# Decay attention, mixture of experts and bilinear layer on one core: where y is summed, where the T sums are formed, how 64-bit weights are staged

## The chip, the cores and the metric

One NeuronCore of a Trainium2 chip runs the whole chain. The metric is device time in microseconds (us) of the core. The engines are PE (matrix products, with PEld its weight loads), DVE (vector), ACT (scalar), POOL (GpSimd) and SP, which here issues nearly all DMAs. Each engine works through its own instructions in the order in which the program gives them; semaphores order the engines against each other.

## The reference

```python
attn_out = _attn_ref(q, k, v, lam)                 # (2, 8, 768, 64), blocked decay attention
x = attn_out.transpose(0, 2, 1, 3).reshape(1536, 512)
# mixture of experts, E = 4, F = 1024: w1 (4, 512, 1024), w2 (4, 1024, 512)
p = domain_probs / (domain_probs.sum(-1, keepdims=True) + 1e-09)
for e in range(4):
    out += p[:, e:e+1] * (np.maximum(x @ w1[e], 0.0) @ w2[e])
# bilinear layer: w1, w2 (512, 1024), w3 (1024, 1024), w_out (1024, 512)
h = (x @ w1) * (x @ w2) @ w3
return h @ w_out
```

`w1`, `w2`, `w3` and `w_out` of the last layer come as 64-bit floats (`1.0 / np.sqrt(...)` makes them so), all else as 32-bit.

## The kernel before

**Numbers in two parts.** Every operand of a product is split into a high part (fp32r, an ACT cast) and a low part (what is left, a DVE subtract), and each product is three matmuls: high by low, low by high, high by high (`products`, L111). A matmul is 128x128 weights by 512 columns.

**Three groups of tokens.** The 1536 tokens are three groups of 512 (`TG`). Hidden units are taken in 32 blocks `k` of 128 (`NJ`), 8 for each expert.

- Attention runs first, with the first blocks of group 0 mixed in; the order is the list `ORDER`, which ends with block 7 in hand.
- **Phase one** (loop at L922) takes group 0 through blocks `k` = 8 to 29: `moe_in(k)` (12 matmuls into bank 4 + k % 3), `moe_z` (DVE), `moe_high` (ACT), then `moe_out(k-2)` (12 matmuls into banks 0 to 3, where group 0's y is summed), `moe_low` (DVE). Blocks 30 and 31 are mixed into the first passes of phase two.
- **Phase two** (loop at L940) takes groups 1 and 2 together, two blocks (a pair `n`) in each pass `m`. Seven products of Strassen's kind (`MULT`, L712) of 6 matmuls each stand for the eight that two groups by two blocks would need. They use sums of x (`x_sums`, L641, POOL, once) and the **T sums** of w1 (`pair_sums`, L661, four POOL instructions for a pair). Between the products stand eight packs of 6 matmuls that bring the hidden units to y. Even passes serve group 1 or 2 in turn (`pass_packs`, L779): four y banks (0 to 3) are summed over two pairs and then added by DVE to a sum in SBUF (`to_sum`, L806), or copied the first time. Products use banks 4 to 6 as chains A, B, C, bank 7 is the w bank in phase one.
- **Gates and the rest** (L968 on): (x w1) * (x w2) of the last layer, again with Strassen-like products for groups 1 and 2 (`quad`), and then by W = w3 w_out (`final`).

**64-bit weights** are converted by hand (`begin64`, `bits64`, `end64`, L228 to L249): two ACT passes, three DVE passes, one POOL add, then the split. The 24 tiles of w_out and w3 are converted in phase one, four w_out tiles, eight w3 tiles, and again, and `w_block` (L588) makes W by 12 matmuls a tile into bank 7: the first eight blocks are copied out by ACT (`w_part`), the second eight added to them by DVE (`w_sum`, L600) and stored in DRAM. The raw tile comes through the pool `raw` of three buffers that all weights share, the converted one through `cv` of two.

**The order of work around the change** is a table of steps: `at_step(t, rank, what, call)` puts a call at position `t`, and `step(t)` emits it there. In phase one 100 units of `t` are one block `k`, in phase two 100 units are a pass and one unit one product or pack. A call that names a tile (`what`) frees a raw buffer, and the next tile of `stream` is loaded behind it (`load_next`, L617), so loads stand on SP's queue in the order in which buffers come free.

## Time and profile before

| | |
|---|---|
| runs | 939.7, 943.1, 950.19 us; median 943.1 us |
| profiled execution | 942.55 us, of which the span of the trace is 940.8 us |
| PE, DVE, ACT, POOL busy | 828.4, 562.7, 333.4, 212.2 us |
| DMA | 88.81 MB, mean 94 GB/s |

A busy PE is not PE at its peak: a matmul record lasts some 390 ns while the next begins after 227 ns, and at a lower granted clock it lasts longer. So the count of matmuls in a stretch, not its busy time, says how long it could have been.

### The profile page before, as it was taken

How to read it: one execution, taken by the hardware profiler on the slowest of the kernel's cores; microseconds unless marked ns; L12 is line 12 of the kernel's file. 1: busy time of each engine (PE TensorE's matmuls, PEld its weight loads, DVE VectorE, ACT ScalarE, POOL GpSimd, SP SyncE). 2: the span in 40 equal slices, each digit the busy share in tenths (PEclk: the TensorE clock that was granted, in tenths of full speed). 3: DMA queues.
4: the chain of work that ended last, by engine and by line, in shares of the span. 5: the costliest groups of instructions: out<-in, count | busy, mean ns of one | idle time of the engine just before them, and what ended most of it. 6: DMA issues, size and time to landing. Idle time of an engine off the chain costs nothing.

```text
span 940.8 us, 10423 instructions
## 1 busy us (share of the span) xinstructions
PE 828.4 (88%) x3968; PEld 666.1 (71%) x3968; DVE 562.7 (60%) x803; ACT 333.4 (35%) x574; POOL 212.2 (23%) x175
## 2 busy tenths in 40 slices
PE   8999928779377699999999999999998689999998
PEld 7778816558255488777777777777787478888887
DVE  6653574245542557766776667777766575677610
ACT  4541433334421234544333333343333433244311
POOL 2111251011110122232222222222200041178200
PEclk9999959899787999999999999999999899999999
DMA  7881333223332322433222222222223310100001
GB/s 257 269 283 46 121 114 106 73 90 107 127 114 87 116 86 68 143 95 106 93 90 79 86 82 90 79 90 79 79 79 99 136 57 10 45 1 1 0 38 53
DMA packets 39938, 88.81 MB, mean 94 GB/s; under 512 B 4560, under 2 KB 9936, under 8 KB 39888
## 3 DMA queue, kind: packets, MB, share of 16 engines
q1 hardware_dynamic: 39216, 88.12, 28.7%
q8 instruction: 31, 0.51, 0.2%
q14 instruction: 19, 0.16, 0.1%
q10 hardware_dynamic: 672, 0.03, 0.0%
HBM read 77.62 MB, written 10.51 MB: 94 GB/s over the span
## 4 chain that ended last, share of the span: by engine, by line
PE 49%; DVE 21%; ACT 9%; issue 4%; DMA 3%; POOL 0%; ACTq 0%; POOLq 0%; DVEq 0%
PE y L122 12%; PE h L734 8%; PE o L122 7%; PE w L122 7%; PE ab L122 4%; PE a L1162 4%; PE b L1162 4%; DVE z L749 4%; PE h L122 4%; DVE w L105 3%; DVE zp L758 3%; DVE z L747 2%; ACT zp L754 2%; DMA raw<-in_w3t_dram 2%; DVE cv L219 1%
## 5 line engine op out<-in xcount | busy, mean ns | idle before, releaser
L122 PE MATMUL y<-zp,w 128*128 128x512 f32 x768 | 198.5, 404 | 27.7 <-DVE ya L812 25.4
L122 PEld LDWEIGHTS y<-zp,w 128*128 128x128 f32 x768 | 147.0, 193 | 66.0 <-DVE ya L812 32.6
L226 POOL TENSOR_TENSOR cv<-cv,raw 128x512 uint32<-128x512 uint32 x40 | 53.2, 1331 | 434.5 <-issue 224.6
L754 ACT CAST zp<-z 128x512 fp32r<-128x512 f32 x64 | 39.7, 621 | 186.1 <-DVE z L749 186.1
L122 PE MATMUL w<-wol,w3h 128*128 128x512 f32 x64 | 36.0, 563 | 70.0 <-ACT w3h L102 30.1
L105 DVE TENSOR_TENSOR wl<-raw,wh 128x1024 fp32r<-128x1024 f32 (+1 forms) x33 | 42.8, 1297 | 53.9 <-ACT wh L102 53.9
L122 PEld LDWEIGHTS w<-wol,w3h 128*128 128x128 f32 x64 | 16.8, 263 | 79.9 <-ACT w3h L102 31.0
L316 ACT CAST hh<-z 128x512 fp32r<-128x512 f32 x32 | 19.8, 619 | 139.3 <-DVE z L309 139.3
L758 DVE TENSOR_TENSOR zp<-z,zp 128x512 fp32r<-128x512 f32 x64 | 58.2, 928 | 11.7 <-ACT zp L754 11.6
L122 PE MATMUL o<-w_hi,z 128*128 128x512 f32 (+1 forms) x208 | 60.0, 373 | 0.0
L309 DVE SCALAR_TENSOR_TENSOR z<-h,pb 128x512 f32<-128x512 f32 x32 | 22.0, 688 | 57.0 <-PE h L122 56.7
L122 PE MATMUL y<-hl,wh 128*128 128x512 f32 x128 | 50.7, 396 | 1.1 <-DVE hl L322 1.1
L122 PE MATMUL h<-xl,wh 128*128 128x512 f32 x128 | 51.4, 402 | 0.0
L122 PE MATMUL h<-xh,wl 128*128 128x512 f32 x128 | 50.1, 391 | 0.0
L122 PE MATMUL y<-hh,wl 128*128 128x512 f32 x128 | 50.0, 390 | 0.0
L122 PE MATMUL y<-hh,wh 128*128 128x512 f32 x128 | 49.9, 390 | 0.0
L747 DVE TENSOR_TENSOR z<-h,u 128x512 f32<-128x512 f32 x32 | 21.9, 685 | 45.3 <-ACT u L741 45.3
L102 ACT CAST wh<-raw 128x1024 fp32r<-128x1024 f32 (+1 forms) x33 | 33.6, 1018 | 38.8 <-PE y L122 35.7
L122 PEld LDWEIGHTS o<-w_hi,z 128*128 128x128 f32 x208 | 38.1, 189 | 6.9
L105 DVE TENSOR_TENSOR w<-w,w 128x512 fp32r<-128x512 f32 x32 | 30.7, 960 | 19.4 <-ACT w L102 19.4
L749 DVE SCALAR_TENSOR_TENSOR z<-z,pb 128x512 f32<-128x512 f32 x48 | 40.4, 842 | 1.6
L122 PE MATMUL o<-w_lo,z 128*128 128x512 f32 (+1 forms) x104 | 38.2, 373 | 0.0
(220 smaller groups left out, 1778.8 us busy)
## 6 DMA issues: line engine op xcount, KB each, us to landing
w<-in_w_dram SPq DMA_DIRECT2D x32, 512.0 KB, 4.0
raw<-in_w_dram SPq DMA_DIRECT2D x31, 512.0 KB, 3.8
raw<-in_w3t_dram SPq DMA_DIRECT2D x16, 512.0 KB, 3.2
raw<-in_wab_dram SPq DMA_DIRECT2D x16, 512.0 KB, 3.2
raw<-in_wout_dram SPq DMA_DIRECT2D x8, 512.0 KB, 3.2
ab_dram<-cv SPq DMA_DIRECT2D x16, 256.0 KB, 4.8
ab<-ab_dram SPq DMA_DIRECT2D x8, 512.0 KB, 3.7
kv<-in_kv_dram SPq DMA_DIRECT2D x7, 512.0 KB, 5.4
```

The lines of the kernel that those rows point to most:

```text
L102: act.copy(out=hi, in_=src)
L105: eng.tensor_tensor(out=lo, in0=src, in1=hi.bitcast(F32), op=ALU.subtract)
L122: lambda i=i, a=a, b=b: pe.matmul(ps, a, b, start=(first and i == 0), stop=(last and i == n - 1))
L226: pool.tensor_tensor(out=b, in0=b, in1=raws.pop(("f", i))[:, :, 0], op=ALU.add)
L309: dve.scalar_tensor_tensor(out=z, in0=h_ps.pop(k)[0], scalar=0.0, in1=pb_t[k // KF, 0], op0=ALU.max, op1=ALU.mult)
L316: act.copy(out=hh, in_=h_t[k][0])
L734: pe.matmul(chain_ps[to], w, x, start=begins and j == 0, stop=j == len(seq) - 1, skip_group_check=True,)
L747: dve.tensor_tensor(out=z, in0=src, in1=kept_u[name], op=ALU.add)
L749: dve.scalar_tensor_tensor(out=z, in0=src, scalar=0.0, in1=pb_t[2 * n // KF, PAIR[m]], op0=ALU.max, op1=ALU.mult)
L754: act.copy(out=t[:, 0], in_=z)
L758: dve.tensor_tensor(out=t[:, 1], in0=z_of.pop((m, f)), in1=t[:, 0].bitcast(F32), op=ALU.subtract)
L1162: pe.matmul(t, w, x, start=i == 0 and n in (1, 2, 5), stop=i == len(seq) - 1, skip_group_check=True,)
```

## The change

- **y of one group in PSUM.** In phase two group 1's y is summed in banks 0 to 3 over all 16 pairs (`first_pass`) and split from there once at the end (`first_split`). Group 2's y has banks 4 and 5, first for its column blocks 0 and 1, then for 2 and 3, each time over two pairs, then added in SBUF as before (`second_pass`, in the even passes). The products have banks 6 and 7, two chains A and B. There are 17 passes in place of 18. Passes 0 and 1 have four packs each, the last one twelve and no products. Gates turn through four pairs of banks.
- **T and x sums on DVE.** The T sums are formed in place, and those of the first 8 pairs in phase one: a tile of w1 is loaded into one buffer of its own (`xt`), summed, stored in DRAM, and read back in phase two as one more tile through `raw` (`"t"`). `x_sums` becomes eight half-size DVE instructions.
- **Conversions staged.** The 24 tiles of w_out and w3 have a raw pool (`r64`, 3) and a converted pool (`ct`, 3) of their own and a stream of their own; all of w_out comes first, into tiles that stay. Begin, bits, high, low and the product stand at least 25 units apart. W is summed over both halves in bank 7 (24 matmuls) and copied once by ACT. All 32 blocks of group 0 now go in phase one, which steps every 25 units; casts and subtracts that stood in one call are separate steps, in both phases.

The core of the diff:

```diff
...
-    f64 = []
-    for q in range(2):
-        f64 += [("wo", mt, q, wout[mt]) for mt in range(4 * q, 4 * q + 4)]
-        f64 += [("w3", kt, q, w3t[kt, q]) for kt in range(KF)]
+    f64 = [("wo", mt, mt // 4, wout[mt]) for mt in range(KF)]
+    f64 += [("w3", kt, q, w3t[kt, q]) for kt in range(KF) for q in range(2)]
     f64 += [("ab", i, q, wab[i, q]) for i in range(KF) for q in range(2)]
 
     spill = {
         "w": tc.dram_tile([P, KF, DM], F32, name="w_dram"),
         "ab": tc.dram_tile([KF, P, 2 * DM], F32, name="ab_dram"),
         "y0": tc.dram_tile([P, KD, TG], F32, name="y0_dram"),
+        "t": tc.dram_tile([NJ // 2, P, 2 * DM], F32, name="t_dram"),
...
+            place, tag = (r64_p, "r64") if i < 24 else (raw_p, "raw")
+            t = place.tile([P, 512, 2], U32, tag=tag, name="raw64")
...
+        place, tag = (ct_p, "ct") if i < 24 else (cv_p, "cv")
+        singles[i] = place.tile([P, 512], F32, tag=tag, name="cv")
...
-    cv_p = opened(ctx, "cv", 2)
     early = ExitStack()
-    wp_p = opened(early, "wp")
+    wo_p = opened(early, "wo")
     xs_p = opened(early, "xs")
     ws_p = opened(early, "ws", 2)
+    ct_p = opened(early, "ct", 3)
+    xt_p = opened(early, "xt")
+    r64_p = opened(early, "r64", 3)
...
-        for call in products(ps, pairs):
+        for call in products(w_ps[kt], pairs, first=q == 0, last=q == 1)[6 * half : 6 * half + 6]:
             call()
 
-    def w_sum(kt, q):
-        if q == 0:
-            w_part[kt] = wp_p.tile([P, DM], F32, tag=f"w{kt}", name="w_part")
-            act.copy(out=w_part[kt], in_=w_ps.pop(kt))
-        else:
-            t = ws_p.tile([P, DM], F32, tag="ws", name="w_sum")
-            dve.tensor_tensor(out=t, in0=w_ps.pop(kt), in1=w_part.pop(kt), op=ALU.add)
-            sp.dma_start(out=spill["w"][:, kt], in_=t)
+    def w_sum(kt):
+        w_part[kt] = ws_p.tile([P, DM], F32, tag="ws", name="w_sum")
+        act.copy(out=w_part[kt], in_=w_ps.pop(kt))
+
+    def w_store(kt):
+        sp.dma_start(out=spill["w"][:, kt], in_=w_part.pop(kt))
...
-    SPLIT_A = NJ - 2
-    PAIRS = 100 * SPLIT_A
-    GATES = PAIRS + 100 * (NP + 2)
+    NPRE = 8
+    PAIRS = 100 * NJ
+    GATES = PAIRS + 100 * (NP + 1)
...
+        dve.tensor_tensor(out=x_sum[n][:, d], in0=left[:, d], in1=right[:, d], op=op)
...
+        f = raws["w1", n] if n >= NPRE else early_w1[n]
+        both, b12, b22 = f[:, 0], f[:, 1, : 2 * P], f[:, 1, 2 * P :]
+        t1, t4 = f[:, 0, : 2 * P], f[:, 0, 2 * P :]
+        dve.tensor_tensor(out=both, in0=f[:, 1], in1=both, op=ALU.subtract)
+        dve.tensor_tensor(out=t4, in0=t1, in1=t4, op=ALU.subtract)
+        dve.tensor_tensor(out=b12, in0=b22, in1=b12, op=ALU.subtract)
+        dve.tensor_tensor(out=b22, in0=b22, in1=t1, op=ALU.subtract)
+
+    early_w1 = {}
+
+    def early_load(n):
+        if n < NPRE:
+            t = early_w1[n] = xt_p.tile([P, 2, DM], F32, tag="t", name="w1")
+            sp.dma_start(out=t, in_=w12[2 * n : 2 * n + 2, :, :DM].rearrange("f p c -> p f c"))
+
+    def early_store(n):
+        sp.dma_start(out=spill["t"][n], in_=early_w1.pop(n).rearrange("p q n -> p (q n)"))
...
+        7: ("s3", "t3", "B"),
         3: ("s4", "b22", "A"),
-        4: ("a22", "t4", "C"),
+        4: ("a22", "t4", "B"),
...
+            chain_ps[to] = bank(6 + "AB".index(to), "h")
...
+    def out_pack(g, n, f, half, first, last):
+        zh, zl = z_pair[n, g, f][:, 0], z_pair[n, g, f][:, 1]
+        wh, wl = w2_t[n, f]
+        for d in (2 * half, 2 * half + 1):
+            if first:
+                y_ps[g, d] = bank((d, 4 + d % 2)[g], "y")
+            c = slice(d * P, (d + 1) * P)
+            for call in products(y_ps[g, d], [((wh[:, c], wl[:, c]), (zh, zl))], first=first, last=last):
+                call()
+
+    def first_pass(ns):
+        return [
+            (lambda n=n, f=f, half=half: out_pack(0, n, f, half, n == 0 and f == 0, n == NP - 1 and f == 1), None)
+            for n in ns
+            for f in range(2)
+            for half in range(2)
+        ]
+
+    def second_pass(ns):
+        of = [(n, f) for n in ns for f in (1, 0)]
+        return [
+            (
+                lambda j=j, n=n, f=f, half=half: out_pack(1, n, f, half, j == 0, j == len(of) - 1),
+                (lambda half=half: [to_sum(d, ns[-1] == NP - 1) for d in (2 * half, 2 * half + 1)])
+                if j == len(of) - 1
+                else None,
+            )
+            for half in range(2)
+            for j, (n, f) in enumerate(of)
+        ]
+
+    def to_sum(d, last):
+        if d not in yacc:
+            yacc[d] = h_p.tile([P, TG], F32, tag="hh" if d < 3 else "hl", name="ya")
+            act.copy(out=yacc[d], in_=y_ps[1, d])
+        else:
+            dve.tensor_tensor(out=yacc[d], in0=y_ps[1, d], in1=yacc[d], op=ALU.add)
         if last:
             if d == 0:
-                y_t[g] = features(g, "y")
-            split(yacc[g, d], *y_t[g][d])
+                y_t[2] = features(2, "y")
+            split(yacc[d], *y_t[2][d])
+
+    def first_split():
+        y_t[1] = features(1, "y")
+        for d in range(KD):
+            split(y_ps[0, d], *y_t[1][d])
...
+        at_step(100 * (j - 3) + 60, 0, None, lambda j=j: prep_high(j))
+        at_step(100 * (j - 3) + 76, 0, ("j", j), lambda j=j: prep_low(j))
     for i in range(24):
         what, n, q, _ = f64[i]
-        t = 100 * KF + 50 * (i * 4 // 3) + 100 * (i // 12)
+        t = 808 + 95 * i if i < 8 else 1568 + 68 * (i - 8)
         at_step(t, 3, None, lambda i=i: begin64(i))
-        at_step(t + 50, 2, ("f", i), lambda i=i: bits64(i))
-        at_step(t + 100, 1, None, lambda i=i: end64(i))
+        at_step(t + 50, 2, None, lambda i=i: bits64(i))
+        at_step(t + 75, 9, ("f", i), lambda: None)
+        at_step(t + 125, 3, None, lambda i=i: end64(i, False))
+        at_step(t + 150, 4, None, lambda i=i: end64(i, True))
         if what == "w3":
-            at_step(t + 150, 4, None, lambda n=n, q=q: w_block(n, q))
-            at_step(t + 200, 5, None, lambda n=n, q=q: w_sum(n, q))
-    at_step(1000, 6, None, x_sums)
+            at_step(t + 225, 6, None, lambda n=n, q=q: w_block(n, q, 0))
+            at_step(t + 250, 6, None, lambda n=n, q=q: w_block(n, q, 1))
+            if q:
+                at_step(t + 251, 1, None, lambda n=n: w_sum(n))
+                at_step(t + 325, 9, None, lambda n=n: w_store(n))
...
+        at_step(1800 + 50 * i, 7, None, lambda n=n, d=d: x_sums(n, d))
...
+    for n in range(NPRE):
+        t = 1800 + 120 * n
+        if n == 0:
+            at_step(t - 75, 8, None, lambda: early_load(0))
+        at_step(t, 8, None, lambda n=n: pair_sums(n))
+        at_step(t + 1, 9, None, lambda n=n: early_store(n))
+        at_step(t + 60, 9, None, lambda n=n: early_load(n + 1))
...
+            at_step(t, 1, None, lambda n=n: pair_first(n, False))
+            at_step(t + 2, 1, None, lambda n=n: pair_first(n, True))
+            at_step(t + 2, 2, None, lambda n=n: pair_second(n, False))
+            at_step(t + 3, 1, ("w1", n, 1) if pre else None, lambda n=n: pair_second(n, True))
+            if not pre:
+                at_step(t + 4, 1, None, lambda n=n: pair_sums(n))
+            at_step(t + (4 if pre else 5), 2, None, lambda n=n: pair_split(n, False))
+            at_step(t + 6, 2, ("t", n) if pre else ("w1", n, 1), lambda n=n: pair_split(n, True))
+        at_step(t + 5, 3, None, lambda n=m: pair_out(n, 0, False))
+        at_step(t + 6, 3, None, lambda n=m: pair_out(n, 0, True))
+        at_step(t + 11, 3, None, lambda n=m: pair_out(n, 1, False))
+        at_step(t + 12, 3, ("w2", m), lambda n=m: pair_out(n, 1, True))
...
+        at = t + (2 + 2 * n if n < 4 else 100 + n - 4)
...
+    at_step(t + 9, 0, None, lambda: first_split())
...
-    for k in range(n_in, SPLIT_A):
+    for k in range(n_in, NJ):
         for part in range(2):
             moe_in(k, part, 4 + k % 3)
+            if part == 0:
+                step(100 * k)
         moe_z(k)
         moe_high(k)
-        step(100 * k)
+        step(100 * k + 25)
         if k - 2 >= n_out:
             for part in range(2):
                 moe_out(k - 2, part)
+                if part == 0:
+                    step(100 * k + 50)
         moe_low(k)
-        step(100 * k + 50)
-        if k == 27:
+        step(100 * k + 75)
...
+            fill = left_over(NJ - 2) + left_over(NJ - 1)
+        elif m == NP:
+            tail = second_pass((m - 2, m - 1))
+            fill = tail[:4] + first_pass((m - 1,)) + tail[4:]
+        elif m % 2:
+            fill = first_pass(tuple(n for n in (m - 2, m - 1) if n >= 0))
+        else:
+            fill = second_pass((m - 2, m - 1))
...
+            for at, i in zip((0, 1, 3, 5, 7, 9, 10) if m > 1 else (0, 1, 3, 5, 6, 8, 9), MULT):
...
+            t = bank(((6, 7), (4, 5), (0, 1), (2, 3))[i % 4][q], f"ab{q}")
...
```

## Rows read from the trace of the kernel before

**Rows 1.** The page: busy times; PE and its granted clock in 40 slices.

```profile
PE 828.4 (88%) x3968; PEld 666.1 (71%) x3968; DVE 562.7 (60%) x803; ACT 333.4 (35%) x574; POOL 212.2 (23%) x175
...
PE   8999928779377699999999999999998689999998
...
PEclk9999959899787999999999999999999899999999
```

**Rows 2.** Stages: length, busy us (x instructions) by engine, PEclk, DMA share, GB/s.

```profile
94.00:355.00 261.00, 189.16 (x721) 148.93 (x720) 130.48 (x177) 87.58 (x132) 49.28 (x32) 0.86 0.31 103
355.00:756.00 401.00, 366.17 (x1538) 294.53 (x1537) 280.05 (x387) 150.75 (x258) 87.79 (x77) 0.97 0.29 92
756.00:940.80 184.80, 181.59 (x816) 150.88 (x816) 99.20 (x126) 59.08 (x106) 59.15 (x40) 0.99 0.08 26
```

**Rows 3.** PE's waits, 94 to 355 us: total us, times, longest.

```profile
PE w L122 <- ACT w3h L102: 30.1, 2, 17.5
PE w L122 <- DVE w_sum L606: 19.1, 5, 4.6
PE w L122 <- ACT w_part L603: 16.4, 7, 3.5
```

**Rows 4.** PE's waits after it, 355 to 757 us.

```profile
PE y L122 <- DVE ya L812: 25.4, 17, 2.5
PE ab L122 <- DVE ya L812: 4.7, 1, 4.7
```

**Rows 5.** The chain of waits: start us, us, what.

```profile
755.83 39.81 PE ab L122 x168
795.64 21.76 PE o L122 x96
```

**Rows 6.** DVE groups, 110:352 us: xcount, busy us, mean ns, idle.

```profile
L322 DVE TENSOR_TENSOR hl<-z,hh 128x512 fp32r<-128x512 f32 x18 | 17.3, 963 | 0.8 <-ACT hh L316 0.7
L219 DVE SCALAR_TENSOR_TENSOR cv<-raw,cv 128x512 uint32<-128x512 uint32 x22 | 15.2, 692 | 0.8
L309 DVE SCALAR_TENSOR_TENSOR z<-h,pb 128x512 f32<-128x512 f32 x19 | 13.1, 688 | 46.6 <-PE h L122 46.6
L210 DVE TENSOR_SCALAR cv<-cv 128x512 f32<-128x512 f32 x22 | 11.4, 517 | 0.0
L105 DVE TENSOR_TENSOR w3l<-cv,w3h 128x512 fp32r<-128x512 f32 x16 | 11.0, 689 | 13.2 <-ACT w3h L102 13.2
L214 DVE TENSOR_SCALAR cv<-cv 128x512 uint32<-128x512 uint32 x22 | 9.4, 427 | 0.8
...
L105 DVE TENSOR_TENSOR a22l<-xf,a22h 128x1024 fp32r<-128x1024 f32 x1 | 1.2, 1227 | 2.5 <-ACT a22h L102 2.5
```

**Rows 7.** DVE's time line beside POOL's x sums: start us, us, instruction.

```profile
121.38 3.35 DVE L105 TENSOR_TENSOR wl<-raw,wh 128x1024 fp32r<-128x1024 f32 x1
```

**Rows 8.** DVE's groups, 400 to 700 us (phase two).

```profile
L758 DVE TENSOR_TENSOR zp<-z,zp 128x512 fp32r<-128x512 f32 x53 | 47.9, 923 | 9.6 <-ACT zp L754 9.6
...
L812 DVE TENSOR_TENSOR ya<-y,ya 128x512 f32<-128x512 f32 x48 | 29.7, 680 | 0.0
...
L105 DVE TENSOR_TENSOR wg<-w,wg 128x256 fp32r<-128x256 f32 x13 | 5.4, 419 | 0.0
```

**Rows 9.** PE's time line, phase two: start us, us, instruction [idle <-releaser].

```profile
516.15 2.60 PE L122 MATMUL y<-zp,w 128*128 128x512 f32 x6 [1.82 <-DVE ya L812]
```

**Rows 10.** DMAs: xcount, KB, us to landing; last, of 40:94 us.

```profile
w<-in_w_dram SPq DMA_DIRECT2D x32, 512.0 KB, 4.0
...
ab_dram<-cv SPq DMA_DIRECT2D x16, 256.0 KB, 4.8
...
w_dram<-w_sum SPq DMA_DIRECT2D x8, 256.0 KB, 3.9
...
y_dram<-y SPq DMA_DIRECT2D x4, 256.0 KB, 2.6
...
raw<-in_w_dram SPq DMA_DIRECT2D x5, 512.0 KB, 6.4
```

303 lines of the change are left out of this document (138 added, 165 removed).

## The prediction

> **What bounds the kernel now.** I read the page first, then three stages, then PE's waits in each. The page has PE busy for 88% of the span and its clock below full in many slices [rows 1]; busy time hides both, so I count matmuls. The price of one at full clock is in the chain of waits: 96 matmuls of the last product in 21.76 us [rows 5], 0.2267 us each. By stage [rows 2]:
>
> - 94 to 355 us (phase one from block 8): 721 matmuls would take 163.4 us; it took 261.0. Lost: 97.6 us, at a mean granted clock of 0.86.
> - 355 to 756 us (phase two): 1538 would take 348.7; it took 401.0. Lost: 52.3 us, at 0.97.
> - 756 us to the end: 816 would take 185.0; it took 184.8. Nothing is lost.
>
> So PE's work is the floor, 150 us are lost above it, and the last stage shows that the other engines can keep PE full.
>
> In phase one the three longest waits come to 65.6 us, and all are waits of the product that makes W: for its converted w3 tile, and for bank 7 to be emptied by ACT or DVE [rows 3]. The rest of the 97.6 is mostly the clock, lower after such stops. Conversions stand in one call with their casts, behind other work in ACT's and DVE's queues, on raw buffers shared with everything. In phase two the 17 waits for `ya` (25.4 us) and one of 4.7 at the first gates [rows 4] are y banks that DVE has not yet added out. A stop of 1.82 us is followed by six matmuls in 2.60 us [rows 9] where 1.36 would do, so each costs more than its wait.
>
> **The change part by part.** The number of matmuls stays. So I take off both losses, 97.6 + 52.3 = 149.9 us, and add what I expect to be lost in the new order.
>
> *Conversions staged.* One position unit is worth 1/100 block: 24 matmuls, 5.44 us, and where w3 is converted, every 68 units, also 12 more (2.72 us), so 100 units are 9.44 us. From the low part (t+150) to its product (t+225) are 75 units, 7 us, for one cast and one subtract of 0.69 [rows 6]. From bank 7's copy (t+251) to the next block's first matmul (t+361) are 110 units, 10 us, for one ACT copy. Both waits of [rows 3] should go. The eight `w_sum` adds go (8 x 0.68). New pools cost SP nothing but the first tile, whose buffer is free only when attention's tiles are: I put 3 us, between 0 and one load, 4.0 [rows 10], and it is ACT that waits there.
>
> *DVE in phase one.* After the change: 22 weight subtracts of 1.23, 24 z and 24 low parts of 0.69, 24 conversions of 0.52 + 0.43 + 0.69 + 0.69, 7 x subtracts of 1.23, 8 x sums of 0.69, 8 T sums, the first pair 2.3 us [rows 6]. A T sum is one 128x512 and three 128x256 instructions; the trace has them on POOL only, so I take DVE's subtracts of those shapes, 0.69 + 3 x 0.42 = 1.95 [rows 6, 8]. Sum: 147 us beside 768 matmuls of PE, 174.1 us. The densest part is t = 1800 to 2640, 79 us of PE: 21.9 (weights, z, low) + 28.8 (conversions) + 15.6 (T) + 5.5 + 4.9 = 77 us of DVE. That is 97%, less for the overlap of neighbouring instructions. PE need not stop when DVE is late by less than about 6 us, since hl(k) is used two blocks on; I put 5 us for stops here, between 0 and 20.
>
> *T sums through DRAM.* One buffer: sum, store 512 KB, load 512 KB, next sum, every 120 units, 11.3 us. The sum waits at the head of DVE's queue, and z, low parts and conversions stand behind it; SP's wait for the store holds the weight loads behind it. No row has a store of 512 KB: 256 KB took 2.6, 3.9 and 4.8 us; a load took 4.0, and 6.4 in the busy stretch [rows 10]. The trip is 1.95 + 2.6 + 4.0 = 8.6 us at the least and 1.95 + 9.6 + 6.4 = 18 at the most (a store of twice 4.8). I take 4.8 and 5.0, since traffic here will be high (four 512 KB transfers or so in each 11 us): 11.8 us. Seven trips cost 7 x (11.8 - 11.3) = 3.5, I put 4; ends 0 and 47. The Trainium skill (SBUF — State Buffer, "The DMA setup-cost knee") gives about 2 us fixed plus bytes at 436 GB/s, an estimate of 3.2 us for 512 KB either way. By it the trip is 8.4 us and these 4 us are nothing; the rows above, longer, decide for me.
>
> *POOL relieved.* DVE's 128x1024 subtract of 1.23 took 3.35 us while POOL formed the x sums [rows 7], and in phase two low parts mean 0.92 where 0.69 is their price [rows 8, 6]. With T and x sums on DVE these stretches go; that is in the DVE sums, not counted again.
>
> *Phase two.* A steady pass is 90 matmuls, 20.4 us. DVE has seven z instructions, four low parts, weight subtracts (0.69, 0.42, 1.23, 2 x 0.69) and a conversion (1.64): 13.0 us; an even pass four `ya` adds of 0.68, 15.7; from pair 8 on a T sum, 17.6. All below 20.4. In odd passes no y bank turns at all. In even passes banks 4 and 5 must be added out between half 0 (step 8) and half 1 (step 11), two products or 2.72 us for two adds, 1.36, behind a z that ends about then. Eight turns: I put 0.75 us each with the clock, 6 us. Ends 0 and 30, the latter by today's wait and its slow matmuls, 1.82 + 1.24 + some, 3.7 each [rows 9]. In passes 0 to 6 a fourth tile goes through three raw buffers: w2 is loaded at step 3, when w1 is freed, and cast at step 5, so ACT waits some 2 us for its 4.0 us landing; u copies stand ahead of it and PE has two packs in hand, so nothing. Passes 0 and 1 have 66 matmuls, 15.0 us, for 13 us of DVE in a chain: 2 us each, 4. The last pass drains group 2's second half and the splits under four packs and the first gate: 4 us, 0 to 10.
>
> *Gates.* Four weight preparations move behind the first gate; DVE is busy for 99 of 185 us there, so nothing; four pairs of banks take the 4.7 us wait and the slow start of the gates away.
>
> Sum: 940.8 - 149.9 + (3 + 5 + 4) + (6 + 4 + 4) = 816.9 us of span, and 1.75 outside it (942.55 - 940.8): 819 us. The profiled run stands 0.55 us below the median of 943.1, so against the median I say **820 us**.
>
> **Rivals.**
>
> 1. *The T trip sets the pace* of t = 1800 to 2640. For it: one buffer, a store that must land before the load, DVE at 97%. Against: loads are otherwise 4.0 us. At 15 us a trip, 7 x 3.7 = 26 in place of 4: 842 us. Chance 0.13.
> 2. *Half turns of two y banks.* Before, four banks turned at each pass and PE waited 17 times; now two turn inside a pass. At today's price, 30 in place of 6: 844 us. The Trainium skill (Perfetto Trace Analysis, "Optimizing Tensor Performance", "Matmuls") wants independent groups to rotate through different banks, so that one is emptied while the next is filled; banks 4 and 5 do not. The trace agrees as far as its waits for `ya` go. Chance 0.12.
> 3. *Phase one stays bound by latency.* bank 7 and the one w3 pair stay, and ACT's and DVE's queues stay in order; if waits move to z or hl, half of the 97.6 us is lost again: 868 us. For it: 97% of DVE. Against: from 94 to 118 us, the fifth slice, conversions ran at a closer spacing beside a PE that was full at full clock [rows 1]. Chance 0.12.
> 4. *Slower.* The DVE queue, stopped by each T load, holds z, hl and the conversions, and the 8 pairs come one by one. To lose the 123 us that I expect to win, a trip must take 11.3 + 123/7 = 29 us: a store and a load of 13 us each, twice the longest of [rows 10]. At 32 us it is 820 + 7 x 20 = 960 us. Chance 0.04.
> 5. *It does not do what it says*: the new pools overlay memory whose release comes late, so that the first tiles wait and everything shifts with little gain: half of all losses stay, 893 us; 0.03, and with no gain at all 943 us, 0.02.
>
> **How the numbers follow.** My case has 0.54. Its own range is 806 (its added losses nearly nothing: the floor of 790.9 plus 1.75 is 793, and some stops always remain) to 838. The range of 8 in 10 takes in rivals 1, 2 and 3: 806 to 872. A change below 1% can't be told from none here. Faster by over 1%: 0.54 + 0.13 + 0.12 + 0.12 + 0.03, less something for mishaps of which I know nothing: 0.92; same 0.03; slower 0.05.
>
> **What would show it.** Phase one after attention near 186 us for 768 matmuls at a clock near full; no wait of PE for w3 or bank 7 above 10 us in total; stores and loads of t of 4 to 6 us each and DVE waiting under 1 us for a T load; odd passes of 20.4 us and even ones under 22; no wait for `ya` over 1 us but in even passes; the first gate without a stop. Wrong if PE waits for z's bank or hl in phase one, if DVE's longest releaser there is the DMA of w1, or if PE waits at step 11 of the even passes.

## The result: 802.3 us where 820 was forecast

The changed kernel takes 802.34 us, the median of four runs (801.64 to 803.04); the kernel before, run beside it, took 942.26 us (939.7 to 950.19; a fourth run, 941.42 us, moved its median from 943.1). The ratio is 0.850, with an interval of 0.845 to 0.855. The forecast of a gain through both stages holds; the time lies 18 us below the forecast and 4 us below the low end of its range, 806.

### The profile after

The page of the kernel after, its span, busy times, and PE's slices and clock, against [rows 1]:

```profile
span 801.3 us, 10423 instructions
...
PE 788.7 (98%) x3968; PEld 645.3 (81%) x3968; DVE 554.0 (69%) x835; ACT 332.2 (41%) x570; POOL 148.9 (19%) x107
...
PE   9999999999899999999999999999999999999998
...
PEclk9999999999999999999999999999999999999999
```

The count of matmuls is the same 3968. The slices that were below 9 in [rows 1], eight between the sixth and the fourteenth and three near the 32nd, are gone but for one, the eleventh, at 8, and so is the lower clock. DVE, which got POOL's sums, is busy for 554 us, no longer than before. In phase two its low parts of z, 0.92 us in the mean of [rows 8], are back at their price, by the page's row after:

```profile
L800 DVE TENSOR_TENSOR zp<-z,zp 128x512 fp32r<-128x512 f32 x64 | 44.1, 689 | 17.9 <-ACT zp L796 16.5
```

That is not the T sums' move alone. With only them on DVE, in the kernel before (a run below), the same low parts still mean 0.87 us; and in the kernel after the low parts of w2 mean 1.15. By DVE's groups, 400 to 600 us, of that run and then of the kernel after:

```profile
L758 DVE TENSOR_TENSOR zp<-z,zp 128x512 fp32r<-128x512 f32 x39 | 33.2, 868 | 6.9 <-ACT zp L754 6.9
```

```profile
L105 DVE TENSOR_TENSOR w<-w,w 128x512 fp32r<-128x512 f32 x20 | 22.9, 1147 | 2.7 <-ACT w L102 2.7
```

The only work that POOL has there in either is its add for the conversion. It now falls beside another DVE instruction than before.

The stages of the kernel after (length, busy us and instructions of PE, PEld, DVE, ACT and POOL, PEclk, DMA share, GB/s), cut at the first high by high matmul of phase two and at the first gate, against [rows 2]:

```profile
93.90:279.00 185.10, 177.94 (x772) 145.20 (x771) 154.30 (x216) 89.56 (x137) 39.66 (x24) 0.99 0.56 187
279.00:611.90 332.90, 332.90 (x1463) 273.59 (x1462) 240.05 (x371) 142.26 (x242) 31.64 (x16) 1.00 0.36 117
611.90:801.30 189.40, 185.95 (x841) 154.20 (x839) 106.83 (x137) 64.56 (x113) 61.55 (x40) 1.00 0.10 35
```

By the price of [rows 5], 0.2267 us, and the kernel's own counts (768, 1464 and 840; the records at the cuts differ by a few), the floors are 174.1, 331.9 and 190.4 us. So phase one loses 11.0 us, phase two 1.0, and the rest is 1.0 shorter than its count. (Phase two's first matmul stands 0.45 us ahead of the cut: cut there, it is 10.6 and 1.5.) Before, 97.6 and 52.3 us were lost. The rest can be shorter than its count because 48 of its matmuls have only 256 columns and follow each other after 0.12 us; by that its floor is some 5 us lower, here as in [rows 2], and what it spends above it is mostly the 3.2 us behind the last matmul.

PE's waits over the whole span (total us, times, longest), against [rows 3, 4]:

```profile
PE w L122 <- ACT w_sum L614: 5.2, 3, 3.2
PE w L122 <- DVE w3l L105: 1.9, 2, 1.5
```

The 65.6 us of waits for w3 and bank 7 are 7.1; the 17 waits for `ya` and the one at the first gate are gone altogether.

The chain of waits after (start us, us, what): the last four packs of passes 4, 5, 8 and 9, and the end of phase two:

```profile
364.73 5.44 PE y L122 x24
...
385.13 5.44 PE y L122 x24
...
446.62 5.48 PE y L122 x24
...
467.20 5.44 PE y L122 x24
...
590.34 21.76 PE y L122 x96
612.10 43.08 PE ab L122 x190
```

From pass 4 on these packs stand 20.40 to 20.58 us apart, where 90 matmuls are 20.4: 20.40 in passes without a T sum, 20.53 to 20.58 in those with one; the last 96 y matmuls take exactly the 21.76 us of [rows 5], and the gates begin at the moment they end.

### The profile page after: what moved, and what is told of

It reads as the page before. It is cut to its first block, busy times and chain, and to the rows that moved or that the text cites. A ratio compares the mean times of both kernels' runs of the same rounds, so it can differ in the third digit from the quotient of the medians.

```text
span 801.3 us, 10423 instructions
## 1 busy us (share of the span) xinstructions
PE 788.7 (98%) x3968; PEld 645.3 (81%) x3968; DVE 554.0 (69%) x835; ACT 332.2 (41%) x570; POOL 148.9 (19%) x107
## 4 chain that ended last, share of the span: by engine, by line
PE 80%; DVE 12%; DMA 5%; issue 1%; ACT 1%; SPq 0%; POOL 0%; ACTq 0%; DVEq 0%; POOLq 0%
PE y L122 27%; PE h L776 19%; PE o L122 8%; PE h L122 5%; PE ab L122 5%; PE a L1236 5%; PE b L1236 5%; DMA w<-in_w_dram 3%; DVE wl L105 2%; PE a L525 2%; PE a L442 2%; DVE hl L331 2%; PE a L519 1%; PE w L122 1%; DVE w3l L105 1%
## 5 line engine op out<-in xcount | busy, mean ns | idle before, releaser
L122 PE MATMUL y<-zp,w 128*128 128x512 f32 x768 | 186.3, 389 | 0.0
L122 PEld LDWEIGHTS y<-zp,w 128*128 128x128 f32 x768 | 144.0, 188 | 30.3 <-ACT ya L855 0.2
L227 POOL TENSOR_TENSOR cv<-cv,raw 128x512 uint32<-128x512 uint32 x40 | 71.3, 1782 | 434.2 <-DVE cv L220 402.2
L800 DVE TENSOR_TENSOR zp<-z,zp 128x512 fp32r<-128x512 f32 x64 | 44.1, 689 | 17.9 <-ACT zp L796 16.5
L789 DVE TENSOR_TENSOR z<-h,v 128x512 f32<-128x512 f32 x16 | 11.0, 690 | 43.5 <-ACT wf L102 29.4
L318 DVE SCALAR_TENSOR_TENSOR z<-h,pb 128x512 f32<-128x512 f32 x32 | 21.9, 685 | 18.8 <-PE h L122 18.3
L122 PE MATMUL h<-xh,wh 128*128 128x512 f32 x128 | 34.8, 390 | 0.0
L791 DVE SCALAR_TENSOR_TENSOR z<-z,pb 128x512 f32<-128x512 f32 x48 | 33.2, 692 | 1.7
L331 DVE TENSOR_TENSOR hl<-z,hh 128x512 fp32r<-128x512 f32 x32 | 28.8, 900 | 5.2 <-ACT hh L325 5.2
```

The source lines that it names most:

```text
L122: lambda i=i, a=a, b=b: pe.matmul(ps, a, b, start=(first and i == 0), stop=(last and i == n - 1))
L227: pool.tensor_tensor(out=b, in0=b, in1=raws.pop(("f", i))[:, :, 0], op=ALU.add)
L318: dve.scalar_tensor_tensor(out=z, in0=h_ps.pop(k)[0], scalar=0.0, in1=pb_t[k // KF, 0], op0=ALU.max, op1=ALU.mult)
L331: dve.tensor_tensor(out=hl, in0=z, in1=hh.bitcast(F32), op=ALU.subtract)
L791: dve.scalar_tensor_tensor(out=z, in0=src, scalar=0.0, in1=pb_t[2 * n // KF, PAIR[m]], op0=ALU.max, op1=ALU.mult)
L800: dve.tensor_tensor(out=t[:, 1], in0=z_of.pop((m, f)), in1=t[:, 0].bitcast(F32), op=ALU.subtract)
```

## The experiments

Times are medians of four runs (ten for the x sums on DVE); the ratios are to the kernel before, run beside each (its medians were 935 to 942 us). The kernel after was not run beside them, so a difference of 1 or 2 us from its 802.3 says little. "Phase one" is the length from 93.9 us to the first high by high matmul of phase two in the profiled execution; it is 185.1 us in the kernel after, and its floor is 174.1.

### The T sums in phase one

**A control.** One buffer fewer for the raw 64-bit tiles, which the next experiment needs for its room.

```diff
-    r64_p = opened(early, "r64", 3)
+    r64_p = opened(early, "r64", 2)
...
```

> The changed kernel with two raw buffers for the 64-bit tiles in place of three; the control of the next run. The changed kernel took 802.3 us with a span of 801.3. Theory A (what is lost in phase one is lost to the round trip of the single T buffer, whose sums start 12.4 us apart where 11.3 were planned): two buffers still leave 61 position units, some 5.7 us, for a load of 3.3 to 3.8 us, so 802 to 804. Theory B (DVE, busy for 17 to 20 of each 20 us from 100 to 240 us, is the bound): 802 to 804 too. Rival C (the own raw buffers are what keeps phase one fed): over 810.

803.6 us (ratio 0.856, 0.850 to 0.863), phase one 186.2 us. That is 1.3 us more, within the spread of the runs (802.4 to 804.6): the third buffer is worth next to nothing.

**Two buffers for the T tiles** (and the control's edit), so that the next tile of w1 is loaded 120 units earlier.

```diff
-    xt_p = opened(early, "xt")
+    xt_p = opened(early, "xt", 2)
...
-        at_step(t + 60, 9, None, lambda n=n: early_load(n + 1))
+        at_step(t - 60, 9, None, lambda n=n: early_load(n + 1))
```

> The run before plus a second T buffer, each load issued 60 units ahead of the sum before it, so that a sum no longer waits for a store and a load in a row. Theory A (round trip): the sums start 11.3 us apart or less, the waits of DVE for the w1 load go, 5 to 8 us off its control, 795 to 798. Theory B (DVE is the bound): no change within 1.5 us, because the sums themselves stay. Theory D (the DMA traffic of that stretch, 210 to 260 GB/s, is the bound): no change either, with longer landings.

802.3 us (0.855, 0.849 to 0.862); phase one 182.0 us, 4.2 less than the control, span 3.9 less, but the median only 1.3 less and its runs spread over 800.3 to 804.0. The first and last T sum of the kernel after, and of this one (min/median/max ns, first and last start):

```profile
L682 DVE TENSOR_TENSOR w<-w x8: 679/692/1211, 157.0 to 243.8; 128x512 f32<-128x512 f32 x8
```

```profile
L682 DVE TENSOR_TENSOR w<-w x8: 679/684/1206, 156.8 to 239.7; 128x512 f32<-128x512 f32 x8
```

Seven steps of 12.4 us become seven of 11.8. In the kernel after DVE waited 4.6 us for these loads, five times (a row below); here not at all. So the trip through one buffer costs 1 to 4 us, and the larger figure is from one profiled execution; this study does not settle it closer.

**All T sums but the first pair back in phase two**: `NPRE = 1` in place of 8.

> T sums of pair 0 alone in phase one, those of the other 15 pairs on DVE in phase two, no trip through DRAM for them. Theory A and B both take the stretch from 1800 to 2640 to its 79 us: 6 to 8 us less there. Theory E (phase two has no wait because its DVE is light): passes 0 to 6 get a T sum of 1.95 us, 13.0 + 1.95 and 15.7 + 1.95 of 20.4 us, still no wait, so 794 to 797 in all. Rival (the waits come back as DVE fills, by 1 us and more in each even pass): 800 to 806.

798.1 us (0.851, 0.845 to 0.857): phase one 176.1 us, 9 less; but phase two 336.9, 4 more. Some 3 us of that come in passes 0 to 2, where PE waits once for ACT's u copy (0.9 us) and once for DVE's z (0.7); the passes behind them take 20.54 in place of 20.40. The time lies 1 us above the range expected and below the rival's: the gain is there, and a loss, though not the wait in each even pass that the rival had.

**All eight sums in phase one, but every 160 units.**

```diff
-        t = 1800 + 120 * n
+        t = 1800 + 160 * n
...
-        at_step(t + 60, 9, None, lambda n=n: early_load(n + 1))
+        at_step(t + 100, 9, None, lambda n=n: early_load(n + 1))
```

> T sums 160 units apart in place of 120, loads 100 units behind the sum: 15 us for a trip of about 12.4, and DVE's work of that stretch spread over 1120 units. Theory A: no wait for the load, 5 to 8 us less, 794 to 797. Theory B: a part of it, 797 to 800. If something else holds phase one: 802.

796.2 us (795.99 to 796.81; ratio 0.849, 0.841 to 0.856), phase one 178.2. DVE still waits three times for a tile of w1 (140 to 260 us), 3.5 us in all, so it is hardly those waits that went. The place alone is worth 6 us; the kernel runs below the one after in each of its four runs.

**Three sums, 300 units apart**: `NPRE = 3`, `t = 1800 + 300 * n`, the load at `t + 225`.

> The kernel after with three T pairs formed in phase one, 300 units apart (28 us), the other 13 in phase two. e4 (every 160 units, eight pairs) was 796.2 us with phase one at 178.2 us, e3 (one pair) 798.1 with phase one at 176.1 and phase two 4 us longer in its passes 0 and 1. If DVE's load and the wait for the T tile make up what is left in phase one, this has phase one at 176 to 178 us and passes 0 and 1 without a wait: 792.5 to 795.5 us. If the residue is the 64-bit conversions themselves, it stays at 795.5 to 798.

796.4 us (796.39 to 796.49; ratio 0.849, 0.844 to 0.854). Its stages:

```profile
93.90:270.50 176.60, 175.13 (x777) 144.55 (x772) 147.60 (x196) 90.07 (x137) 40.71 (x24) 1.00 0.51 167
270.50:605.00 334.50, 334.06 (x1464) 273.19 (x1463) 253.45 (x390) 141.86 (x241) 32.12 (x16) 1.00 0.33 108
```

Phase one is 176.6 us, as the theory of DVE's load had it, 2.5 above the floor, at full clock. The time lies 0.9 us above that theory's range and inside the rival's, because phase two is 1.6 us longer than in the kernel after, not because of phase one. So of the 11.0 us that phase one loses, 6.9 go when all eight T sums stand 160 units apart, and 8.5 when only three are formed there, 300 apart. Spread sums thin out DVE's load and the DMA traffic at once; which of the two counts is not shown. Both this and the 160-unit version beat the kernel after by 6 us; they cannot be told apart.

### The staging of the conversions

**One raw pool for all weights again** (three buffers, one stream of loads; the converted tiles keep theirs).

```diff
-            place, tag = (r64_p, "r64") if i < 24 else (raw_p, "raw")
+            place, tag = raw_p, "raw"
...
```

> The changed kernel, but the 24 tiles of w_out and w3 come through the pool raw of three that all weights share, in one stream, as before the change; the spacing of the steps stays. Changed kernel: 802.3 us, phase one from block 8 to the first product of phase two 185.1 us. Theory F (the spacing of the steps, not the own buffers, ended the waits of phase one): a load is still issued about one block before its use, so 802 to 808. Rival C (own buffers did it): phase one loses 30 us and more, over 830.

813.1 us (0.870, 0.865 to 0.874), phase one 194.2. Own buffers are worth 10.8 us (9.1 by phase one): more than the view that they do nothing, less than the view that they are the heart of it.

**The conversion's last steps close together again**: both parts split in one call at t+100, both halves of the product at t+150, the copy at t+200.

```diff
-        at_step(t + 125, 3, None, lambda i=i: end64(i, False))
-        at_step(t + 150, 4, None, lambda i=i: end64(i, True))
+        at_step(t + 100, 1, None, lambda i=i: (end64(i, False), end64(i, True)))
...
-            at_step(t + 225, 6, None, lambda n=n, q=q: w_block(n, q, 0))
-            at_step(t + 250, 6, None, lambda n=n, q=q: w_block(n, q, 1))
+            at_step(t + 150, 6, None, lambda n=n, q=q: w_block(n, q, 0))
+            at_step(t + 150, 6, None, lambda n=n, q=q: w_block(n, q, 1))
...
```

> The changed kernel with its own buffers, but the conversion's end as before the change: cast and subtract in one call 50 units behind the bits, the 12 matmuls in one piece 50 units behind that, the copy and the store 50 units later; begin and spacing from tile to tile as changed. Theory F: the cast waits for POOL, the subtract for the cast, PE for both, and each stop lowers PE's clock, so phase one grows by 25 to 60 us, 827 to 862. Rival C: under 810, since the loads come in time.

813.5 us (0.870, 0.865 to 0.875), phase one 194.8. The spacing is worth 11.1 us (9.7 by phase one), far less than I expected.

**Both.**

> Both of the two runs before: the shared raw pool and the close steps, with the rest of the change as it is (finer steps of phase one, W summed in one chain, T sums, phase two). If the two do not act on each other, the sum of their losses, by theory F 30 to 70 us, 832 to 872. The kernel before lost 97.6 us in this phase; what is left to that sum is then due to the denser old positions of the conversions and to the separate casts and subtracts of the weights.

824.3 us (0.882, 0.877 to 0.886), phase one 205.6: the two costs add up, 21.9 us. What PE waited for longest in this one:

```profile
PE w L122 <- ACT w3h L102: 11.2, 2, 11.0
```

The stop at the first w3 tile is back, one wait of 11.0 us, though shorter than in [rows 3].

### y in PSUM

**Group 1's y added to a sum in SBUF in each odd pass**, as in the kernel before, with the change's banks and order kept.

```diff
-            (lambda n=n, f=f, half=half: out_pack(0, n, f, half, n == 0 and f == 0, n == NP - 1 and f == 1), None)
+            (
+                lambda n=n, f=f, half=half: out_pack(0, n, f, half, n == ns[0] and f == 0, n == ns[-1] and f == 1),
+                (lambda half=half: [to_sum1(d) for d in (2 * half, 2 * half + 1)]) if n == ns[-1] and f == 1 else None,
+            )
...
```

> The changed kernel, but group 1's y is not held in PSUM over all pairs: banks 0 to 3 are summed over one odd pass and then added to a sum in SBUF by DVE, four adds of 0.68 us in each odd pass, as before the change. Theory G (the waits of phase two went because no bank is wanted again within a pass or two of being filled, whoever empties it): banks 0 to 3 are wanted again two passes on, 20 us, DVE has 13.0 + 2.7 us of 20.4, so 801.5 to 804, no wait for ya in odd passes. Rival H (to hold y in PSUM is itself what won phase two): the waits of 1 to 2 us and the slow matmuls come back in 8 passes, 815 to 832.

802.3 us (0.859, 0.854 to 0.863), span 800.1, no wait for `ya` but one of 0.2 us. Keeping y in PSUM over all pairs wins nothing by itself: four banks that no one asks for until two passes later may be added out at leisure. What is left for the gain is that a group's banks are its own, and the order of the passes; of these only the order is tried, next.

**The two halves of banks 4 and 5 next to each other** in the even passes: their products move behind them, so that no product stands between the last pack of half 0 and the first of half 1.

```diff
-            for at, i in zip((0, 1, 3, 5, 7, 9, 10) if m > 1 else (0, 1, 3, 5, 6, 8, 9), MULT):
+            for at, i in zip(((0, 1, 3, 5, 7, 9, 10) if m % 2 else (0, 1, 3, 5, 7, 10, 12)) if m > 1 else (0, 1, 3, 5, 6, 8, 9), MULT):
```

> The changed kernel with the two products that stood between the halves of group 2's y in even passes moved behind them, so that banks 4 and 5 are wanted again right after the last pack of half 0. By theory G the cover of 2.72 us is what makes the turn free: now PE waits at each of the 7 even passes for an add of 0.68 us behind a z of 1.4, 1.5 to 2.5 us each and slow matmuls at times, 12 to 26 us more, 814 to 828. Rival (the turn is free anyway, since DVE is idle when half 0 ends): 802 to 806.

822.6 us (0.878, 0.873 to 0.882), 20.3 more than the kernel after.

```profile
PE y L122 <- DVE ya L857: 13.5, 6, 2.5
...
PE y L122 <- ACT ya L855: 2.8, 1, 2.8
```

A wait in each of the seven even passes is back, some as long as the longest of [rows 4], and 16.3 us of them cost 20. Two products, 2.72 us, between the two halves are what makes the turn free.

### The kernel before with one part changed

**The x sums on DVE.**

```diff
-            pool.tensor_tensor(out=x_sum[n], in0=left, in1=right, op=op)
+            dve.tensor_tensor(out=x_sum[n], in0=left, in1=right, op=op)
```

> The kernel before with one thing changed: its x sums, four instructions of 128x1024 that POOL took 2.6 to 3.2 us each for, on DVE (about 1.23 us each). Theory J (these POOL sums, beside which DVE's instructions lasted 2.6 to 3.4 us and behind which the conversion's POOL add stood, made the stop of 17.5 us at 118 to 136 us): the stop goes, 15 to 25 us less with the clock, 915 to 928 beside 943. Rival (the stop is the order of the first w3 conversions, whoever sums x): within 6 us of the kernel before.

938.2 us against 938.8 (0.999, 0.995 to 1.002): nothing. The longest stop falls only from 17.5 to 14.8 us: POOL's x sums are not what makes most of it.

**The T sums on DVE**: the four instructions of `pair_sums`, `pool.` made `dve.`.

> The kernel before with one thing changed: the T sums of phase two on DVE (1.95 us a pair) in place of POOL (some 4.5 us a pair). If POOL's use of the port that DVE needs was a part of phase two's loss, low parts go from 0.92 to 0.69 us and waits for ya shrink: 5 to 15 us less, 928 to 938. If DVE's added work weighs more, ya comes later: 943 to 955. Theory G says that the y banks decide: within 8 us of the kernel before.

919.0 us (0.979, 0.975 to 0.983), 20 less, more than expected. Of the 25.4 us of waits for `ya` in [rows 4], 9.0 are left:

```profile
PE y L122 <- DVE ya L812: 9.0, 16, 2.6
```

**Bank 7's copy in the same step as its block**, 50 units earlier.

```diff
-            at_step(t + 200, 5, None, lambda n=n, q=q: w_sum(n, q))
+            at_step(t + 150, 5, None, lambda n=n, q=q: w_sum(n, q))
```

> The kernel before with one thing changed: bank 7 is emptied (w_part, w_sum) right behind its 12 matmuls, 50 units earlier. Theory K (the 35.5 us of waits for w_part and w_sum are the copy's late place in ACT's and DVE's queues): these waits go, 20 to 45 us less with the clock, 898 to 923. Rival (the wait moves: ACT and DVE now stand in their queues until PE has done the block, and z, casts and conversions behind them come late): within 10 us of the kernel before, with more waits for w3 in their place.

886.2 us (0.945, 0.940 to 0.949): this one line wins 52.5 us, more than a third of what the whole change does. PE's longest waits in 94 to 355 us, and then the stage, against [rows 3, 2]:

```profile
PE w L122 <- ACT w3h L102: 29.7, 2, 17.2
PE w L122 <- DVE w_sum L606: 4.2, 2, 2.1
```

```profile
94.00:301.60 207.60, 171.70 (x723) 138.88 (x723) 128.47 (x177) 88.25 (x132) 50.14 (x32) 0.91 0.39 129
```

The twelve waits for bank 7, 35.5 us, are two of 4.2. The stage is 53 us shorter for the same matmuls. Some 36 us of that are waits (these, and 4.4 us for ACT's `wh`); the other 17 are PE's busy time, 189.2 before and 171.7 here, and the granted clock, 0.86 before, is 0.91. The two stops at a w3 tile stay.

**Both edits.**

> The kernel before with both edits that won alone: bank 7's copy right behind its block (e11, -52 us) and the T sums on DVE (e10, -20 us). Theory (the first is a loss of phase one, the second of phase two, and they do not touch): 862 to 872 us. Rival (with phase one faster, DVE gets the T sums and the same z work closer together, or T on POOL was already hidden once phase one is faster): 874 to 890 us.

866.5 us (0.923, 0.918 to 0.929): 72.7 less, where 52.5 and 19.8 are 72.3. The two losses add up.

### The two stops at a w3 tile

What stood ahead of the first stop can be read in the run with bank 7's copy moved: PE, then ACT (start us, us, instruction [idle <-releaser]).

```profile
135.76 0.79 PE L122 MATMUL w<-wol,w3h 128*128 128x512 f32 x1 [17.18 <-ACT w3h L102]
```

```profile
128.93 0.62 ACT L316 CAST hh<-z 128x512 fp32r<-128x512 f32 x1 [8.75 <-DVE z L309]
129.74 0.62 ACT L102 CAST woh<-cv 128x512 fp32r<-128x512 f32 x1 [0.20 <-POOL cv L226]
133.02 0.68 ACT L200 ACTIVATE cv<-raw 128x512 f32<-128x512 f32 x1 [2.67 <-DMA raw<-in_w3t_dram]
...
135.08 0.63 ACT L102 CAST w3h<-cv 128x512 fp32r<-128x512 f32 x1
```

The cast that PE wants stands behind the fourth w_out tile's cast, and behind the first pass over the next raw tile, whose load came late. Ahead of them ACT itself stood 8.75 us for a z of DVE. Either it is a backlog, or the order of ACT's queue whatever the distance.

**The block 50 units later**, `w_block` at `t + 200` in place of `t + 150`.

> The kernel before; only the step that makes W moves, from t+150 to t+200, so that it stands 100 units behind the conversion's last call and bank 7's copy stands right behind it (as in e11_before_w_copy_early, whose block stays at t+150). That run kept PE's two waits for a converted w3 tile, 29.7 us. Theory L (those two stops are the conversion chain being late by a few us at the first two w3 tiles, and 50 units more absorb them): the two waits fall below 12 us in all, the time is 862 to 875 us, 11 to 25 below e11's 886. Rival M (the chain's lateness is not a matter of distance: ACT's cast stands behind something that ends only once PE goes on): the waits stay above 22 us and the time is 880 to 892 us.

905.9 us (0.964, 0.956 to 0.971), and PE waited six times for a w3 cast, 36.0 us in all. A w3 tile's place in the pair is reused by the tile after next; where those are 100 units apart, that cast now came ahead of the block, so some products took the wrong w3 tile and had to wait for its later cast. The run says nothing on the question.

**Room behind the first four w_out tiles**, with bank 7's copy moved as above: all later conversions, with their products, 150 units later.

```diff
-        t = 100 * KF + 50 * (i * 4 // 3) + 100 * (i // 12)
+        t = 100 * KF + 50 * (i * 4 // 3) + 100 * (i // 12) + 150 * (i >= 4)
```

> The kernel before with bank 7's copy right behind its block (e11, 886.2 us) and every conversion behind the first four w_out tiles 150 units later, its products with it. e13 could not tell theory L from rival M: with the block 50 units on, the cast into one of the two places of the w3 pair came to stand ahead of the product of the tile before in that place in some cases, so parts of W were made of the wrong w3 tile and PE waited for a later cast. Here every distance inside a conversion stays. Theory L (a backlog: the four w_out tiles, that no product needs at once, fall behind PE by their loads through the shared raw buffers, and the first w3 product has to wait for all of it): with 150 units between, the first stop of 17.2 us falls below 6 us, the second of 12.5 stays: 869 to 877 us. Rival M (the cast of a w3 tile stands on ACT's queue behind the first pass over a tile whose load comes late, whatever the distance): both stops stay above 10 us and the time is 880 to 890 us.

879.7 us (0.938, 0.932 to 0.943). **Room behind both fours**, also with the copy moved, `100 * (i >= 4) + 50 * (i >= 16)`:

> As e17_before_gap_one, but 100 units behind the first four w_out tiles, and 50 more behind the second four. Theory L: both stops shrink, the first from 17.2 to under 9 us, the second from 12.5 to under 10, the time is 866 to 876 us. Rival M: both stops stay above 10 us, 880 to 890 us.

879.1 us (0.938, 0.933 to 0.943). PE's waits for w3 and for `hl` in the first of these two runs, and for w3 in the second:

```profile
PE w L122 <- ACT w3h L102: 14.3, 2, 10.2
PE y L122 <- DVE hl L322: 8.8, 3, 4.3
```

```profile
PE w L122 <- ACT w3h L102: 16.6, 2, 8.8
```

By stop, the first goes from 17.2 to 4.1 us with 150 units and to 8.8 with 100; the second, from 12.5, to 10.2 with no more room and to 7.8 with 50. The stops shrink with the room, so they are a backlog. The time fell by 7 only, to 3 us above the range of the backlog in both: with PE running on, its waits for `hl` rise from 1.1 to 8.8 and 6.8 us. The first of them is for an instruction that lasted 2.82 us beside POOL's x sums, where 0.69 is its price; from DVE's time line in the first of the two runs:

```profile
119.27 2.82 DVE L322 TENSOR_TENSOR hl<-z,hh 128x512 fp32r<-128x512 f32 x1
```

A latency taken away at one place showed up at the next. So the x sums may have cost nothing only because a longer stop covered them; on DVE together with the moved copy and the room they were not tried.

### The T sums on POOL in the new order

The kernel after with one pair ahead (`NPRE = 1`) and, from the second pair on, the four instructions of `pair_sums` on POOL.

> The kernel after with T sums of one pair ahead (as e3_t_in_phase_two, 798.1 us) and those of the other 15 pairs formed by POOL in phase two, as the kernel before did. If POOL's adds beside DVE were harmful by themselves, as in the kernel before (20 us there), the time is 808 to 820 us with waits of PE for ya or z. If they were harmful only because four y banks turned at every pass, so that now DVE has slack, the time is 796 to 801 us with under 3 us of PE waits in phase two. A T tile that comes late from POOL would show as a wait of PE for t.

809.7 us (0.863, 0.857 to 0.869), 11.6 above the same kernel with them on DVE. PE's waits in phase two, then DVE's time line in one pass (its three conversion instructions and T's low part), then POOL's at the same time:

```profile
PE h L776 <- DVE z L789: 9.7, 13, 1.7
```

```profile
418.03 1.30 DVE L211 TENSOR_SCALAR cv<-cv 128x512 f32<-128x512 f32 x1 [0.17 <-ACT cv L201]
419.37 0.85 DVE L215 TENSOR_SCALAR cv<-cv 128x512 uint32<-128x512 uint32 x1
420.25 1.11 DVE L220 SCALAR_TENSOR_TENSOR cv<-raw,cv 128x512 uint32<-128x512 uint32 x1
423.08 1.24 DVE L105 TENSOR_TENSOR wt<-w,wt 128x1024 fp32r<-128x1024 f32 x1 [1.72 <-ACT wt L102]
```

```profile
417.75 1.30 POOL L682 TENSOR_TENSOR w<-w 128x512 f32<-128x512 f32 x1 [15.90 <-DVE wf L105]
419.13 0.80 POOL L683 TENSOR_TENSOR w<-w 128x256 f32<-128x256 f32 x1
```

The three DVE instructions of the conversion take 3.26 us; with the T sums on DVE they take 1.54, 0.43 and 0.69 for the second and third as in [rows 6], and for the first, in the 300-unit run:

```profile
412.32 0.42 DVE L211 TENSOR_SCALAR cv<-cv 128x512 f32<-128x512 f32 x1
```

And the sums themselves take 4.1 us on POOL (the two shown, 0.92 and 1.07) where DVE needs 1.95. PE's waits are for the z that stands behind T's split on DVE's queue. In this pass the later T is what delays it: DVE, done with the slower conversion at 421.36, stood 1.72 us for T's cast, which waited for POOL's last sum. Sums on POOL cost time in the new order too, without any wait for DVE to empty a y bank.

## Why the prediction was right on the way and off in the size

**The floor and the two losses** were right. Predicted for the span: 790.9 us (the 94 us ahead as they were, and the matmuls behind) and whatever stops remain. The counts of the kernel after give 790.3.

**The step that failed is the phase two sum, 6 + 4 + 4.** It measured 1.0 us (1.5 from its first matmul) where 14 were put; that is 13.0 of the 15.6 us between 816.9 and 801.3. The waits were expected in the right places; that DVE would not get done in time there was wrong. Term by term:

- *Eight half turns, 0.75 us each*: nothing. The working had the answer, two products or 2.72 us for adds of 1.36, and then charged something between it and today's wait. (That wait's price was also put too high: the record of six matmuls is longer than their share of PE by the last one's overlap, so 2.60 us of [rows 9] are 1.1 more than normal, not 1.24.) With the two products taken away the turns cost 20 us, so they are a full cover, not part of one.
- *Passes 0 and 1, 4 us*: under 0.5, and the T sums in phase one are the reason: with them back in phase two, passes 0 to 2 take some 3 us more.
- *The last pass, 4 us*: nothing; the chain runs from y into the gates without a gap.

**The same error set the range's low end.** 806 was argued as the floor and "some stops always remain". But the lower ends that the terms had of their own, nothing for all but passes 0 and 1, add up to 797 us, so the measured 802.3 lies inside the working and outside the range drawn from it. The last stage of the kernel before lost next to nothing [rows 2]; with DVE busy for 99 of its 185 us it does not prove the same for passes with 13 to 18 of 20.4, but with 3 us of DVE to spare in each, near zero was at least as likely as the 14.

**Phase one, 3 + 5 + 4 = 12**, measured 11.0, right in sum. Its parts: the first tile cost nothing, since PE is never idle up to 140 us:

```profile
93.90:140.00 46.10, 46.10 (x206) 38.16 (x205) 41.64 (x55) 27.35 (x43) 12.65 (x8) 1.00 0.55 183
```

The T sums stood 12.4 us apart where 11.8 were forecast, which holds PE's own stops too; the cost of the trip was 1 to 4. Of the 6.9 to 8.5 us that go with the T sums spread, some 3 to 7 are then left for what the forecast called DVE's stops and put at 5. "97% of the densest 79 us" was the right place to look: from the first T sum on, DVE is busy for 71.6 of 79 us (91%), and PE does 318 matmuls, 72.1 us:

```profile
157.00:236.00 79.00, 74.34 (x318) 60.06 (x317) 71.59 (x108) 38.99 (x62) 18.05 (x11) 0.98 0.69 236
```

How the trip reaches PE can be read at its longest stop, 3.2 us, in the chain of waits: the load ends, the T sum follows on DVE, then z, behind it ACT's copy of bank 7, and then the product.

```profile
211.75 5.58 DMA w<-in_w_dram
...
219.37 0.61 DVE z L318
...
220.53 0.59 ACT w_sum L614
...
221.16 2.93 PE w L122 x6
```

**The reason given for the loss before** holds only in part. Both waits of [rows 3] went, and more than the waits, as the clock term said. But "staged" was one word for four things. The copy's place in its queue is worth 52 us in the kernel before; buffers of their own and the spacing between steps are 11 each, undone in the kernel after; the x sums' engine nothing, tried alone. The 52 belong to the old order: in the run with the close steps the copy stands 50 units behind its block again, and all that this run undoes is 11 us. What makes the rest of the difference (half as many copies, finer steps) was not tried.

**The rivals.** The T trip as pace (842) was out: DVE waited 4.6 us for it (140 to 260 us), and the run without such waits is only 1 to 4 us shorter:

```profile
DVE w L682 <- DMA w<-in_w_dram: 4.6, 5, 2.0
```

Phase one bound by latency (868) is how the kernel before behaves with its stops relieved one by one, with waits turning up at `hl`; with all parts together it did not. The slower case and the two in which the change wins little or nothing are out by the time itself.

The half turns (844) took place only in the order that puts the halves together. The Trainium skill (Perfetto Trace Analysis, "Optimizing Tensor Performance", "Matmuls") wants independent groups to rotate through banks; here two banks alternate with themselves and cost nothing, with two other products between, and 20 us without. So the traces agree with the rule's reason, that the emptying needs other matmuls to hide under, more than with a need for further banks.

**What would show it**, of the list: phase one near 186 (185.1), waits for w3 and bank 7 below 10 us (7.1), odd passes 20.4 and even ones under 22 (20.40 to 20.58), no `ya` wait, first gate without a stop: all seen. DVE was to wait under 1 us for a T load and waited 4.6, up to 2.0 at a time; and one sign of being wrong came true from 140 to 260 us, the DMA of w1 as DVE's longest releaser (the row above is the first of its list), though over all of phase one DVE waits longer, 11.7 us, for ACT's casts of weights. Loads of w1 took 4.9 us in the stretch, in the forecast 4 to 6; stores, and loads of the T tiles (3.7 us by the page), were put too long. The DMAs of 140 to 260 us:

```profile
w<-in_w_dram SPq DMA_DIRECT2D x9, 512.0 KB, 4.9
t_dram<-w SPq DMA_DIRECT2D x8, 512.0 KB, 3.0
```

Here the Trainium skill's estimate (SBUF — State Buffer, "The DMA setup-cost knee"), 3.2 us for 512 KB, was nearer for the stores than the 4.8 us that I took from stores of half the size. For the loads in that stretch it was too short: they took 4.9, and DVE waited for five of them.

## What to carry to other kernels

When an engine's in-order queue empties a bank that PE needs next, look first at where that emptying stands in the queue, and move it right behind the product: one line won 52 us here in the old order, and new buffers or another engine for the sums won 11 to 20. Count the matmuls of a stage, and where the sum of each other engine's work in a pass leaves it some us to spare, let the range of the loss begin at zero. A cover that is longer than the work under it covered all of it here; test it by taking it away.

## What the runs showed of the hardware that I had not expected

DVE's one-input instructions slow down beside POOL as well as those with two inputs: `cv<-cv` took 1.30 and 0.85 us where 0.42 and 0.43 are the price, in the run with T on POOL and with T on DVE. In phase two of the kernel after the only POOL work left is one add for each conversion, and DVE's low part of w2 beside it still means 1.15 us, where the run with T on DVE in the old order has 0.69.

The Trainium skill (SBUF — State Buffer, "SBUF: two separate sides") has the two engines share a port pair that one of them holds for a whole instruction. The trace of the kernel after agrees where one instruction can be followed. DVE's T sum and the POOL add that it met:

```profile
180.07 1.21 DVE L682 TENSOR_TENSOR w<-w 128x512 f32<-128x512 f32 x1 [0.88 <-DMA w<-in_w_dram]
```

```profile
179.42 1.31 POOL L227 TENSOR_TENSOR cv<-cv,raw 128x512 uint32<-128x512 uint32 x1 [3.50 <-ACT w3h L102]
```

The add ends at 180.73; the sum then takes 0.55 us more, a little less than its own 0.69, so it was held nearly, not wholly, until then.

A long stop costs more than its wait. In the run with bank 7's copy moved, before the first stop, in it, and just behind it (columns as in the stages):

```profile
105.00:118.00 13.00, 13.00 (x59) 10.74 (x59) 8.29 (x12) 5.90 (x10) 5.28 (x4) 1.00 0.49 152
118.00:135.70 17.70, 0.58 (x3) 0.16 (x1) 14.05 (x13) 5.53 (x9) 11.56 (x6) 0.65 0.25 87
135.70:141.00 5.30, 4.69 (x11) 3.43 (x12) 3.40 (x6) 1.17 (x4) 1.29 (x1) 0.55 0.51 183
```

PE was full at full clock; the granted clock fell while it stood, and for the 5.3 us after the stop it is 0.55 in the mean, near the lower of the two levels (1.2 of 2.4 GHz). In them PE stood another 0.6 us and did the 12 matmuls of the block, which are 2.7 us at the price of [rows 5], so the lower clock cost some 2 us more than the waits.
